# Loading the 128 remainder rows of two weight matrices in sixteen pieces of 15 down to 1 and 8 partitions instead of one piece of 128

## The chip, the cores and the metric

The kernel runs on one core of one Trainium2 chip. The metric is the device time of one execution in microseconds. Each profile is of one execution, and its span (first to last instruction) is some 1.8 us shorter than the device time.

## The reference

Two branches are computed from the same two normalised tokens and added: attention of one new token over the last 2048 positions of a cache (16 key/value heads, 32 query heads, two sequences), and a two-layer MLP with a squared ReLU.

```python
# x [2, 1, 576]; k_cache, v_cache [2, 16, 8192, 128]; wq [576, 4096]; wo [4096, 576]; w1 [576, 4608]; w2 [4608, 576]; all bf16
xn = _layernorm(x)
# branch A
q = (xn @ wq) ...                      # 32 heads of 128
k, v = caches[:, :, Sk - W:, :]        # W = 2048
o = softmax(q k^T / sqrt(128)) v;  A = o @ wo
# branch B
h = relu(xn @ w1 + b1) ** 2;       B = h @ w2 + b2
return x + A + B
```

Some 53.6 MB are read from HBM, the chip's main memory, for two tokens of output, so this is above all a program of loads.

## The kernel before

The inner size 576 is 4 x 128 + 64. The first 512 rows of `wq` and `w1` load as four tiles of 128 rows each. The last 64 rows are folded: each row is cut in two halves, which gives 128 half rows of 2048 elements (wq, 4096 bytes) or 2304 elements (w1, 4608 bytes), one for each of the 128 partitions of SBUF, the memory on the chip that the engines compute from. This folded tile is "the remainder", `wq_rem` and `w_rem` in the profile.

```python
    def issue_kv(tiles, cache, u, name, parts=1):
        tl = kvpool.tile([P, UE], BF16, tag="kv", name=f"{name}_{u}")      # 2 MiB, six buffers
        ...
        return [lambda i=i: nc.sync.dma_start(out=tl[:, i * n:(i + 1) * n], in_=v[:, :, i * n:(i + 1) * n]) ...]

    def issue_w(tiles, wt, c, name, width, lrem):
        if c < NFULL:
            tl = wbig.tile([P, WBW], BF16, tag="wbig", name=f"{name}_{c}")
            nc.sync.dma_start(out=tl[:, 0:width], in_=wt[c * P:(c + 1) * P, :])
        else:
            tl = wrem.tile([P, WRW], BF16, tag="wrem", name=f"{name}_rem")
            nc.sync.dma_start(out=tl[:, 0:lrem], in_=wt[NFULL * P:D, :].rearrange("r (s l) -> (r s) l", s=S))
        tiles[c] = tl
```

Nearly all loads are issued by one engine, SP (`nc.sync`), in this order at the start:

```python
    k0 = issue_kv(k_tiles, A_k_cache, 0, "k", parts=2)
    issue_wq(0); k0[0](); issue_wq(1); k0[1]()
    for c in range(2, KC):        # wq_2, wq_3, then the remainder
        issue_wq(c)
    ...
    load_k(1); issue_w1(0); issue_w1(1); load_v(0); load_k(2)
    for c in range(2, KC):        # w1_2, w1_3, then the remainder
        issue_w1(c)
    load_v(1); issue_wo(0); load_k(3)
```

The framework gives each load a completion semaphore (a counter that tells when the load has landed).

## Time and profile before

| | before |
|---|---|
| device time, median of 2 runs | 137.37 us (137.30 to 137.44) |
| span of the profiled run | 135.6 us |
| packets of the load queue q1, share of 16 engines' span | 94.7%, or 128.4 us of 135.6 |
| the rest of the span (engines idle, or on other queues) | 7.2 us |

The share of a queue, times the span, is the time that an average DMA engine spends in packets of that queue. (A packet is what one engine moves at a time, here one row of one partition: 128 packets of 4096 bytes for the remainder of wq.) 0.947 x 135.6 = 128.4 us. What is left, 7.2 us, holds the start, the end, the instruction fetches and all idleness.

SP's timeline of the kernel before (start, length, line, operation, out<-in, count) around the two remainder loads:

```profile
4.34 0.44 SPq L103 DMA_DIRECT2D wq_rem<-in_A_wq_dram  x1
4.83 0.55 SPq L94 DMA_DIRECT2D k<-in_A_k_cache_dram  x1
10.25 4.59 SPq L100 DMA_DIRECT2D w<-in_B_w_dram  x2
...
21.19 0.42 SPq L103 DMA_DIRECT2D w_rem<-in_B_w_dram  x1
25.88 0.55 SPq L94 DMA_DIRECT2D v<-in_A_v_cache_dram  x1
```

The 2 MiB load of k follows the remainder of wq within 0.5 us, while the engines are still busy with loads from before. And the chain that ended last, by engine (shares of the span):

```profile
DMA 55%; PE 35%; DVE 3%; issue 2%; POOL 1%; ACT 1%; SPq 1%; POOLq 0%; ACTq 0%
```

SP's own issuing is 1% of that chain. And one line of SP's waits (engine and line, releaser: total us, times, longest):

```profile
SPq L94 <- DMA v<-in_A_v_cache_dram: 8.6, 2, 4.3
```

Line 94 issues the k and v loads. So even before the change, some loads wait until an earlier load has landed.

### The profile page before, as it was taken

The page shows a single profiled execution, that of the slowest core. Times are in us where ns is not written, and L with a number is a line of the kernel's source. Part 1 is how long each engine was busy: PE and PEld are TensorE (multiplying, and loading weights), DVE is VectorE, ACT ScalarE, POOL GpSimd, SP SyncE. Part 2 cuts the span into 40 slices and gives each one's busy share as a digit, 9 for nine tenths or more (in the row PEclk, how much of TensorE's full clock was granted, in tenths as well). Part 3 has the DMA queues.
Part 4 walks back from the last instruction along what each step waited for, and adds up shares of the span by engine and source line. Part 5 has one row for each costly group of instructions (what it writes and reads, how often), then busy time and mean ns, then how long its engine had stood idle before and what let it go on. Part 6 is the DMA issues. An engine that isn't in the chain of part 4 may idle for free.

```text
span 135.6 us, 4461 instructions
## 1 busy us (share of the span) xinstructions
PE 102.5 (76%) x2054; PEld 91.9 (68%) x2054; DVE 53.9 (40%) x124; ACT 43.0 (32%) x47; POOL 10.0 (7%) x31
## 2 busy tenths in 40 slices
PE   1049947599968999879943993999399599768961
PEld 0039947589968999839933993688399479664530
DVE  7502421574352325422653446355634645660001
ACT  6705550165012521004701550272155127110000
POOL 6400000110110001100011001101100110110000
PEclk9999985569855685556985698698559959955599
DMA  5999999999999999999999999999999999999940
GB/s 112 418 419 418 428 442 402 420 429 440 430 393 430 438 411 409 444 425 396 440 440 406 445 420 425 404 443 423 425 430 413 430 415 426 422 410 417 393 166 1
DMA packets 5278, 53.90 MB, mean 397 GB/s; under 512 B 630, under 2 KB 652, under 8 KB 1164
## 3 DMA queue, kind: packets, MB, share of 16 engines
q1 hardware_dynamic: 5188, 53.61, 94.7%
q8 instruction: 16, 0.26, 0.8%
q0 software_dynamic: 64, 0.01, 0.0%
q14 instruction: 2, 0.02, 0.0%
q10 hardware_dynamic: 8, 0.00, 0.0%
HBM read 53.62 MB, written 0.00 MB: 395 GB/s over the span
## 4 chain that ended last, share of the span: by engine, by line
DMA 55%; PE 35%; DVE 3%; issue 2%; POOL 1%; ACT 1%; SPq 1%; POOLq 0%; ACTq 0%
DMA k<-in_A_k_cache_dram 41%; PE kT_ps L237 18%; DMA w<-in_B_w_dram 10%; PE hT_ps L323 5%; DMA b_sb<-in_B_b_dram 4%; PE sc_ps L252 4%; PE out_ps L213 4%; PE oT_ps L289 3%; PE qT_ps L225 1%; ACT kT L240 1%; POOL b_sb L146 1%; DVE l L271 1%; DVE sub L266 1%; SPq L94 0%; DVE fin_sb L414 0%
## 5 line engine op out<-in xcount | busy, mean ns | idle before, releaser
L237 PE MATMUL kT_ps<-ident,k 128*128 128x128 bf16 x512 | 47.3, 260 | 9.9 <-DMA k<-in_A_k_cache_dram 9.9
L237 PEld LDWEIGHTS <-k 128*128 128x128 bf16 x512 | 39.6, 119 | 11.8 <-DMA k<-in_A_k_cache_dram 10.7
L240 ACT COPY kT<-kT_ps 128x1024 bf16<-128x1024 bf16 x32 | 32.3, 1012 | 40.1 <-PE kT_ps L237 40.0
L242 DVE COPY kT<-kT_ps 128x1024 bf16<-128x1024 bf16 x32 | 22.0, 690 | 33.4 <-PE kT_ps L237 33.4
L252 PE MATMUL sc_ps<-qT_all,kT 128*128 128x8 bf16 x512 | 21.6, 168 | 1.6 <-ACT kT L240 0.8
L252 PEld LDWEIGHTS <-kT 128*128 128x128 bf16 x512 | 19.1, 100 | 2.6 <-ACT kT L240 1.2
L289 PE MATMUL oT_ps<-pT,v 128*128 128x8 bf16 x512 | 15.5, 167 | 1.9 <-issue 1.4
L269 ACT ACTIVATE pT<-sub 128x512 bf16<-128x512 f32 x8 | 5.0, 630 | 35.1 <-DVE sub L266 35.1
L289 PEld LDWEIGHTS <-v 128*128 128x128 bf16 x512 | 14.4, 99 | 2.1 <-issue 1.6
L271 DVE TENSOR_REDUCE l<-pT 128x8 f32<-128x512 bf16 x8 | 8.5, 1066 | 4.2 <-ACT pT L269 4.2
L213 PE MATMUL out_ps<-wo,ws 128*2 128x288 bf16 x64 | 8.3, 438 | 2.4 <-DVE ws L309 2.4
L323 PE MATMUL hT_ps<-xnT,w 128*128 128x2 bf16 x144 | 9.8, 201 | 0.0
L323 PEld LDWEIGHTS <-w 128*128 128x128 bf16 x144 | 9.4, 165 | 0.0
L258 DVE TENSOR_REDUCE m<-sc_ps 128x8 f32<-128x512 f32 x8 | 5.5, 692 | 9.7 <-PE sc_ps L252 9.7
L262 POOL PARTITION_ALL_REDUCE gmax<-m x8 | 2.9, 364 | 84.8 <-DVE m L260 84.8
L213 PE MATMUL out_ps<-w,hT_sb 128*2 128x288 bf16 x72 | 6.9, 353 | 1.3 <-DMA w<-in_B_w_dram 1.3
L213 PEld LDWEIGHTS <-ws 128*2 128x2 bf16 x64 | 3.5, 115 | 5.4 <-DVE ws L309 2.8
L213 PEld LDWEIGHTS <-hT_sb 128*2 128x2 bf16 x72 | 3.8, 103 | 4.3 <-issue 1.9
L266 DVE TENSOR_TENSOR sub<-sc_ps,gm 128x512 f32<-128x512 f32 x8 | 5.5, 692 | 0.3
L225 PE MATMUL qT_ps<-xnT,wq 128*128 128x2 bf16 x128 | 4.0, 165 | 2.2 <-DMA wq<-in_A_wq_dram 1.9
L225 PEld LDWEIGHTS <-wq 128*128 128x128 bf16 x128 | 3.9, 103 | 2.2 <-DMA wq<-in_A_wq_dram 2.0
L273 POOL PARTITION_ALL_REDUCE lsum<-l x8 | 3.2, 398 | 24.5 <-DVE l L271 24.5
(58 smaller groups left out, 35.1 us busy)
## 6 DMA issues: line engine op xcount, KB each, us to landing
v<-in_A_v_cache_dram SPq DMA_DIRECT2D x8, 2048.0 KB, 28.4
k<-in_A_k_cache_dram SPq DMA_DIRECT2D x7, 2048.0 KB, 29.4
w<-in_B_w_dram SPq DMA_DIRECT2D x4, 1152.0 KB, 17.7
wo<-in_A_wo_dram SPq DMA_DIRECT2D x4, 1152.0 KB, 27.4
wq<-in_A_wq_dram SPq DMA_DIRECT2D x4, 1024.0 KB, 6.9
w<-in_B_w_dram SPq DMA_DIRECT2D x3, 1296.0 KB, 22.7
k<-in_A_k_cache_dram SPq DMA_DIRECT2D x2, 1024.0 KB, 9.1
w<-in_B_w_dram SPq DMA_DIRECT2D x1, 864.0 KB, 15.7
```

The costliest lines, as they stand in the source:

```text
L213: nc.tensor.matmul(out_ps[32 * i:32 * i + B, :], lhsT=lhsT, rhs=rhs_of(i * OH, (i + 1) * OH), start=start, stop=stop, skip_group_check=True)
L225: nc.tensor.matmul(qT_ps[:, h, :], lhsT=lhsT, rhs=xnT[:, xc, :], start=(c == 0 and h == 0), stop=(c == KC - 1), skip_group_check=True)
L237: nc.tensor.transpose(out=kT_ps[:, i * P:(i + 1) * P], in_=k_sb[:, j * Dh:(j + 1) * Dh], identity=ident[:])
L240: nc.scalar.copy(out=kT[:], in_=kT_ps[:])
L242: nc.vector.tensor_copy(out=kT[:], in_=kT_ps[:])
L252: nc.tensor.matmul(sc_ps[:, g * JG + i, :], lhsT=kT[:, i * P:(i + 1) * P], rhs=qT_all[:, b, tq * NC:(tq + 1) * NC], start=True, stop=True)
L258: nc.vector.tensor_reduce(out=m1[:], in_=sc_ps[:].rearrange("p j c -> p c j"), axis=AX.X, op=ALU.max)
L266: nc.vector.tensor_tensor(out=sub[:], in0=sc_ps[:], in1=gm2[:].unsqueeze(1).to_broadcast([P, NJ, NC]), op=ALU.subtract)
L269: nc.scalar.activation(out=pT[:], in_=sub[:], func=ACT.Exp, scale=scale)
L271: nc.vector.tensor_reduce(out=l1[:], in_=pT[:].rearrange("p j c -> p c j"), axis=AX.X, op=ALU.add)
L289: nc.tensor.matmul(oT_ps[:], lhsT=v_sb[:, j * Dh:(j + 1) * Dh], rhs=pT_tiles[u][:, j, :], start=(j == 0), stop=(j == NJ - 1))
L323: nc.tensor.matmul(hT_ps[:, s * FR + r, :], lhsT=lhsT, rhs=xnT[:, xc, :], start=(c == 0 and s == 0 and r == 0), stop=(c == KC - 1), skip_g ...
```

## The change

The intent, as I read it, is to give some DMA engines more rows than others: a load of n partitions, n under 16, is spread over n engines, so loads of 15, 14, ... 1 partitions make a staircase if each begins at the same engine. That they do is my assumption. If some engines finish late for another reason, such a staircase could even them out. The bytes and the matmuls stay the same.

```diff
             tl = wrem.tile([P, WRW], BF16, tag="wrem", name=f"{name}_rem")
-            nc.sync.dma_start(out=tl[:, 0:lrem], in_=wt[NFULL * P:D, :].rearrange("r (s l) -> (r s) l", s=S))
+            rem = wt[NFULL * P:D, :].rearrange("r (s l) -> (r s) l", s=S)
+            p0 = 0
+            for n in list(range(15, 0, -1)) + [8]:
+                nc.sync.dma_start(out=tl[p0:p0 + n, 0:lrem], in_=rem[p0:p0 + n, :])
+                p0 += n
```

More of the change, by code (lines that the diff above doesn't have):

```diff
@@ L360 @@
     load_k(3)
-    nxt = {0: [], 1: [], 2: [lambda: load_v(2), lambda: load_k(4)]}
     def step(u, extra=()):
@@ L404 @@
                 load_k(u + 2)
-        if u >= NU - 1:
-            pass
         if u == NU - 1:
```

## The prediction

Passages are cut from the prediction below, and each cut is marked. The sum that the cut terms belong to came to +2.8 us at the end: eight rows of both tensors more for the engine that was assumed to have a row of every piece (8 x 0.33 = 2.6 us), and 30 more semaphore packets of 6 ns (0.2 us). "Engine 0" is that engine; the higher the number of an engine, the fewer of the pieces it was assumed to have, so that engine 8 came out 0.3 us earlier than before and engine 15, with none, 2.6 us. All of this is an assumption. The tiles behind the pieces were put 1.3 us (wq) and up to 2.8 us (w1) later. The packet records of the kernel before show this much: 36 loads of 128 partitions come with 576 semaphore packets, 16 each, and the load of x, of 2 partitions, has two data and two semaphore packets.

> **What bounds the kernel now.** I read the slices of the page first, then the DMA queues, then the chain of waits near the end, then windows around the end, and last the single packet records of the trace. The slices of the kernel before (busy tenths of 40 slices of 3.39 us, and GB/s):
>
> ```profile
> PE   1049947599968999879943993999399599768961
> DMA  5999999999999999999999999999999999999940
> GB/s 112 418 419 418 428 442 402 420 429 440 430 393 430 438 411 409 444 425 396 440 440 406 445 420 425 404 443 423 425 430 413 430 415 426 422 410 417 393 166 1
> ```
>
> The DMA engines are full from the second slice to the thirty-eighth; PE has holes. So the loads set the time, and what I must ask is not "how many bytes" (the change moves the same bytes) but "which of the 16 engines is done last". That is seen at the end. Windows of the kernel before, from 20 us to the landing of the last load (columns: length, busy time and count of PE, PEld, DVE, ACT, POOL, then PE clock, DMA share, GB/s):
>
> ```profile
> 20.00:125.00 105.00, 86.01 (x1813) 79.23 (x1812) 46.07 (x95) 33.17 (x36) 6.10 (x16) 0.71 1.01 423
> 125.00:128.50 3.50, 3.50 (x34) 1.91 (x32) 0.00 (x0) 0.00 (x0) 0.00 (x0) 0.52 0.97 399
> 128.50:131.80 3.30, 2.21 (x36) 1.34 (x32) 0.00 (x0) 0.00 (x0) 0.00 (x0) 1.00 0.52 204
> ```
>
> For 105 us all engines are full at 423 GB/s, which is 26.4 GB/s an engine. Then, in the last 3.3 us, the share is 0.52 and the rate 204 GB/s: half of the engines have nothing left and the other half go on. The finer windows show the step:
>
> ```profile
> 128.00:128.50 0.50, 0.50 (x10) 0.29 (x6) 0.00 (x0) 0.00 (x0) 0.00 (x0) 0.61 0.97 387
> 128.50:129.00 0.50, 0.38 (x8) 0.14 (x3) 0.00 (x0) 0.00 (x0) 0.00 (x0) 1.00 0.68 277
> ...
> 131.00:131.50 0.50, 0.27 (x6) 0.19 (x7) 0.00 (x0) 0.00 (x0) 0.00 (x0) 1.00 0.46 180
> 131.50:132.00 0.50, 0.50 (x12) 0.33 (x7) 0.00 (x0) 0.00 (x0) 0.00 (x0) 1.00 0.19 69
> ```
>
> The program's end hangs on the slower half. The chain of waits, last pieces (start, length, what):
>
> ```profile
> 119.21 13.05 DMA w<-in_B_w_dram
> 132.26 0.04 issue
> 132.30 0.55 PE out_ps L213 x6
> 132.85 0.02 issue
> 132.87 0.45 DVE fin_sb L414
> ```
>
> After the last load lands at 132.26 us only 0.6 us of matmuls and the store remain. So one microsecond on the last engine is one microsecond of the kernel.
>
> Why is one half late, when each load of 128 partitions gives every engine the same bytes? The queue table gives the only other sizeable traffic:
>
> ```profile
> q1 hardware_dynamic: 5188, 53.61, 94.7%
> q8 instruction: 16, 0.26, 0.8%
> ```
>
> 0.8% of 16 x 135.6 us is 17 us for 16 packets, 1.08 us each. In the packet records, one chained to the next by start and end, each of these 16 fetches takes its engine's turn for some 1.06 us and is followed by a slow data packet (1.08 us where 16 KB otherwise takes 0.61), so it costs its engine about 1.5 us. In those records eight chains end between 128.4 and 129.4 us and eight between 131.65 and 131.82: the difference, 3.1 us, is two fetches. So I read: eight engines carry two fetches each, eight carry none. The records don't number the engines. That gap decides this case.
>
> [...]
>
> **The change part by part.** Removed: two loads, of 128 x 4096 bytes (wq) and 128 x 4608 bytes (w1), 8 rows of each on every engine. Added: 16 loads in place of each, of 15, 14, ... 1 partitions and a last one of 8. [...]
>
> One row of both is 8704 bytes, at 26.4 GB/s 0.33 us. [...] Each small load also ends in a 4-byte semaphore packet; they hold an engine for about 6 ns[...].
>
> SP issues 30 more loads. The old remainder issues took 0.44 and 0.42 us; at up to 0.4 us each, 15 more are at most 6 us at each of two places. In the timeline wq's remainder is issued at 4.34 us and lands 16.6 us later, w1's at 21.2 and lands 27.1 us later: the queue ahead of these issues is 16 and 27 us deep, so 6 us of issuing hides and no engine should run dry. All other engines keep their order: the instruction order of PE, DVE, ACT and POOL is the same but for line numbers.
>
> Intermediate waits: [...] The first stretch of the chain waits for a k tile issued at 15.5 us that lands at 41.2 us; the projections have slack there. The last w2 issue, at 119.2 us, has 13 us of queue ahead of it. So these delays shift work but add nothing at the end beyond engine 0's own lateness.
>
> **The rivals.** It comes down to which eight engines carry the fetches.
> - A: engines 8 to 15. The late ones get less: engine 8 ends at 131.7 - 0.3 = 131.4 us. The early ones get more: engine 0 ends at 128.5 + 2.8 = 131.3. Gain about 0.3 us: 137.1 us. For it: someone who unloads high engines may have seen them late[...].
> - B: a set that holds engine 0 (0 to 7, the even ones, or mixed). Engine 0 ends at 131.7 + 2.8 = 134.5: 140.2 us, 2.1% slower. For it: nothing in the trace forbids it. If the lowest of the set is 1 or 2, +7 or +6 rows, 139.5 to 139.9, within 2%.
> - C: the small loads are badly overlapped, SP can't keep the queue full, or the waits between small semaphores add up; a hole of 1 to 3 us in the DMA row near 11 or 28 us would follow, 138.5 to 140 us. The queue depths speak against it.
> - D: a large gain. Ruled out by the sum: if all 16 engines ended together they would end at (128.7 + 131.7)/2 = 130.2, 1.5 us sooner, 1.1%. No order of rows can give 2%.
>
> **Range and chances.** A I hold at about a half, B with engine 0 at a quarter, its milder forms (engines 1 to 7 alone) at 0.15, C at 0.1. A is "same". B with engine 0 lies at 2.1%, on the edge, and is "slower" in somewhat over half; C in a third. That makes slower about 0.2, faster 0.01. The middle of the chances is just above A: 137.5 us. Because the outcomes have two peaks (137.1 and about 140), the range is wide: 136.7 to 140.4.
>
> **What would show it.** Windows over the last 3 us: in A the share falls in a slope instead of a step and the last load lands at about 132.0; in B the share falls to 0.06 to 0.3 for the last 2 to 3 us, since engine 0 and a few neighbours go on alone, and lands near 135. [...] SP's lines should show 32 remainder issues at 0.1 to 0.4 us, and the DMA row should keep its nines. Wrong would be: fetches that move to other engines, [...](a load of 1 partition spread on 16), or a hole in the DMA row.

## The result, and the profile after

The changed kernel takes 151.14 us (150.89 and 151.39, two runs), against 137.37 us. The ratio is 1.0996, 95% interval 1.0956 to 1.1036: 10% slower, far outside the predicted range. (Ratios here and below, with their intervals, are not quite the ratio of the medians that I quote.)

The slices of the changed kernel, 40 of 3.73 us:

```profile
PE   1079722539994999717399179779979879957751
DMA  4999925999999933999999999999999999999930
GB/s 157 412 420 426 342 55 166 404 403 446 422 435 412 350 72 115 404 400 442 422 418 448 426 422 426 431 399 453 422 422 422 422 406 446 408 414 413 408 150 1
```

Two holes stand in the DMA row that was all nines before: slices 6 and 7 (about 18.6 to 26 us) and slices 15 and 16 (about 52 to 60 us). Everywhere else the rate is what it was. The queues:

```profile
q1 hardware_dynamic: 5412, 53.61, 87.6%
q8 instruction: 16, 0.26, 0.7%
```

0.876 x 149.1 = 130.6 us of packets: 2.2 us more than before. The rest is 18.5 us: 11.3 us more. The sum, 13.5 us, is the growth of the span. So the loss is in two terms of very unequal size, and the larger one is idleness. The packet count tells also that the pieces are spread as intended: 5412 - 5188 = 224 packets more. That fits one semaphore packet for each engine that takes part in a load: two loads of 16 made 32, and the pieces make 2 x (15 + 14 + ... + 1 + 8) = 256, which is 224 more. In the packet records the last nine pieces of wq, of 8, 7, ... 1 and 8 rows, begin in groups of 8 (21.35 to 21.41 us), 7 (21.69 to 21.75), 6, 5, 4, 3, 2, 1 and 8 row packets; the packets of each group all overlap in time (those of the first take 258 to 316 ns), so a piece of n runs on n engines.

The first hole in steps of a microsecond (windows of the changed kernel: length, busy time and count of PE, PEld, DVE, ACT, POOL, then PE clock, DMA share, GB/s):

```profile
17.00:18.00 1.00, 0.83 (x33) 0.74 (x30) 0.69 (x1) 0.98 (x2) 0.00 (x0) 1.00 0.92 295
18.00:19.00 1.00, 0.00 (x0) 0.00 (x0) 0.00 (x0) 0.91 (x1) 0.00 (x0) 1.00 0.74 135
19.00:20.00 1.00, 0.00 (x0) 0.00 (x0) 0.00 (x0) 0.00 (x0) 0.00 (x0) 0.65 0.27 74
20.00:21.00 1.00, 0.51 (x19) 0.51 (x19) 0.00 (x0) 0.00 (x0) 0.00 (x0) 0.50 0.01 4
...
23.00:24.00 1.00, 0.00 (x0) 0.00 (x0) 0.00 (x0) 0.00 (x0) 0.00 (x0) 0.50 0.16 53
24.00:25.00 1.00, 0.00 (x0) 0.00 (x0) 0.00 (x0) 0.00 (x0) 0.00 (x0) 0.50 0.92 250
```

In the window from 20 to 21 us the sixteen engines together move 4 GB/s. They have nothing to do. SP's timeline says what SP does in the meantime:

```profile
4.26 19.05 SPq L106 DMA_DIRECT2D wq_rem<-in_A_wq_dram  x16
23.35 0.55 SPq L94 DMA_DIRECT2D k<-in_A_k_cache_dram  x1
...
27.56 30.11 SPq L106 DMA_DIRECT2D w_rem<-in_B_w_dram  x16
57.72 0.55 SPq L94 DMA_DIRECT2D v<-in_A_v_cache_dram  x1
```

Sixteen pieces of wq occupy SP from 4.26 to 23.3 us, and the k load behind them, issued at 4.83 us before, goes out at 23.35 us. Sixteen pieces of w1 take 30 us, and the v load behind them moves from 25.88 to 57.72 us. The issuing is not what takes this long: a piece takes 0.25 to 0.54 us. SP waits, and its list of waits names for what (engine and line, releaser: total us, times, longest):

```profile
SPq L106 <- DMA k<-in_A_k_cache_dram: 13.6, 4, 4.6
SPq L106 <- DMA w<-in_B_w_dram: 11.3, 4, 4.0
SPq L106 <- DMA wq<-in_A_wq_dram: 9.0, 4, 4.4
```

The line that issues remainder pieces waits for other, earlier loads to land. In the kernel before, the remainder line has no such wait in this list. The chain that ended last, by engine, and its pieces around the first hole (start, length, what):

```profile
DMA 68%; PE 17%; SPq 9%; issue 2%; DVE 1%; ACT 1%; POOL 0%; ACTq 0%; POOLq 0%
```

```profile
3.78 16.67 DMA wq<-in_A_wq_dram
20.46 0.27 SPq L106
20.73 0.04 issue
20.78 0.29 SPq L106
...
23.04 0.27 SPq L106
23.31 0.04 issue
23.35 0.55 SPq L94
```

SP has gone from 1% to 9% of the chain. The chain reads: the last big load of wq lands at 20.46 us; only then SP may issue nine more pieces, one every 0.32 us; only after them comes k. Between 18 and 24 us there is nothing left in the engines' queues but those pieces.

The end, which the prediction was about, costs hardly more than it did, but its shape is another. Windows of the changed kernel:

```profile
142.00:142.50 0.50, 0.00 (x0) 0.00 (x0) 0.00 (x0) 0.00 (x0) 0.00 (x0) 1.00 0.65 263
143.00:143.50 0.50, 0.50 (x14) 0.36 (x9) 0.00 (x0) 0.00 (x0) 0.00 (x0) 1.00 0.42 166
143.50:144.00 0.50, 0.27 (x6) 0.06 (x1) 0.00 (x0) 0.00 (x0) 0.00 (x0) 1.00 0.20 69
144.50:145.00 0.50, 0.39 (x8) 0.28 (x9) 0.00 (x0) 0.00 (x0) 0.00 (x0) 1.00 0.18 69
```

Before, the DMA share stood near 0.5 for two microseconds and then fell; here it slopes down, and about three engines (0.18 of 16) go on alone until 145 us. What the share lacks to 1, summed over half microseconds, is 1.8 us from 128 to 132 us before and 1.9 us from 141 to 145 us here. Neither sign that the prediction gave for its cases A and B can be read from this shape: the kernel with even pieces below (e3) ends in the same way, with 0.64, 0.60, 0.30, 0.12, 0.12 and 0.11 in the half microseconds from 144 to 147 us.

### The profile page after: what moved, and what is told of

The parts are those of the page before. It is cut to its first block, busy times and chain, and to the rows that moved or that the text cites. A ratio compares the mean times of both kernels' runs of the same rounds, so it can differ in the third digit from the quotient of the medians. Undisturbed runs are those within 1.5% of the kernel's fastest.

```text
span 149.1 us, 4499 instructions
## 1 busy us (share of the span) xinstructions
PE 103.3 (69%) x2054; PEld 93.9 (63%) x2054; DVE 54.2 (36%) x124; ACT 43.2 (29%) x47; POOL 10.0 (7%) x31
## 3 DMA queue, kind: packets, MB, share of 16 engines
q1 hardware_dynamic: 5412, 53.61, 87.6%
## 4 chain that ended last, share of the span: by engine, by line
DMA 68%; PE 17%; SPq 9%; issue 2%; DVE 1%; ACT 1%; POOL 0%; ACTq 0%; POOLq 0%
DMA k<-in_A_k_cache_dram 29%; DMA w<-in_B_w_dram 28%; DMA wq<-in_A_wq_dram 11%; PE kT_ps L241 11%; SPq L106 3%; PE sc_ps L256 3%; SPq L94 2%; PE oT_ps L293 2%; SPq L100 2%; PE out_ps L217 2%; SPq L127 1%; ACT kT L244 1%; DVE sub L270 0%; DVE fin_sb L415 0%; POOL gmax L266 0%
## 5 line engine op out<-in xcount | busy, mean ns | idle before, releaser
L241 PE MATMUL kT_ps<-ident,k 128*128 128x128 bf16 x512 | 49.5, 267 | 13.6 <-DMA k<-in_A_k_cache_dram 13.6
L241 PEld LDWEIGHTS <-k 128*128 128x128 bf16 x512 | 41.5, 123 | 15.5 <-DMA k<-in_A_k_cache_dram 14.5
L256 PEld LDWEIGHTS <-kT 128*128 128x128 bf16 x512 | 19.7, 101 | 2.2 <-ACT kT L244 1.0
L217 PE MATMUL out_ps<-w,hT_sb 128*2 128x288 bf16 x72 | 5.4, 299 | 2.8 <-DMA w<-in_B_w_dram 2.8
L217 PEld LDWEIGHTS <-hT_sb 128*2 128x2 bf16 x72 | 3.3, 89 | 4.9 <-issue 3.4
```

The lines of the kernel that those rows point to most:

```text
L217: nc.tensor.matmul(out_ps[32 * i:32 * i + B, :], lhsT=lhsT, rhs=rhs_of(i * OH, (i + 1) * OH), start=start, stop=stop, skip_group_check=True)
L241: nc.tensor.transpose(out=kT_ps[:, i * P:(i + 1) * P], in_=k_sb[:, j * Dh:(j + 1) * Dh], identity=ident[:])
L256: nc.tensor.matmul(sc_ps[:, g * JG + i, :], lhsT=kT[:, i * P:(i + 1) * P], rhs=qT_all[:, b, tq * NC:(tq + 1) * NC], start=True, stop=True)
```

## The experiments

**The first theory** (T1, "lanes", in the expectations). The list of the built program's SP instructions shows, behind each load, the completion semaphore that it waits for:

```
DMACopy wq_rem 15x2048
DMACopy wq_rem 14x2048   waits DMAHW0
DMACopy wq_rem 13x2048   waits DMAHW1
...
DMACopy wq_rem  8x2048   waits DMAHW6      <- the semaphore of wq_3, the last big load
DMACopy wq_rem  7x2048   waits DMAHW7
...
DMACopy k      128x8192  waits DMAHW7
```

The loads that SP and ACT issue take eight semaphores in turn, and a load can be issued only when the load eight places before it has landed. So at most eight loads are in flight. (The traces of both kernels agree: the records of these loads name eight semaphores in turn, and in the changed kernel the eighth piece, issued at 20.46 us, waits for that of wq_3, which landed then.) Eight big ones are 16 us of work or more (in the kernel before, the remainder of wq lands 16.6 us after its issue); eight pieces are next to nothing. When 16 pieces stand in a row, the eighth must wait for the last big load, and by then the engines are empty. This wait is not in the diff: the framework puts it in.

The rivals at first were the uneven rows themselves, and a fixed cost of each small load. The uneven rows come in two sizes: T2, that they cost some 13 us, in proportion to rows, and T3, the +2.8 us of the prediction. Later experiments brought in a second effect, called T4 below. Passages are cut from the expectations, and marked. Other letters or numbers in the texts are explained by the sentence in which they stand.

Every kernel below gave a correct result. All times are medians of four runs, and the kernel before ran in the same rounds on the same chip (137.34 to 137.41 us).

### One remainder at a time

```diff
-            for n in list(range(15, 0, -1)) + [8]:
+            for n in (list(range(15, 0, -1)) + [8] if name == "wq" else [P]):     # e1; e2: "w1"
```

> Only wq's remainder is cut into 16 loads; w1's is one load as before. Theory T1 (each load of the queue waits for the landing of the load eight places earlier, so 16 small loads in a row let the big loads drain and leave the DMA engines empty for some 5 us at each of the two places): one hole near 18 to 24 us, none near 53 us, 143 us (142 to 145). Rival T2 [...]: 47% of the loss by bytes, 143.5 us, but with no hole and a longer tail. Rival T3 (the prediction's sum for the imbalance alone): 137 to 138.8 us.

> Only w1's remainder is cut. T1: no hole near 20 us, one hole of some 5 us near 45 to 55 us, 143 us (142 to 145), and the excesses of e1 and e2 add up to about the whole 13.8 us. T2: 53% of the loss, no hole. T3: 137 to 138.9 us.

Measured: 144.44 us with wq alone cut (ratio 1.0517, 1.0501 to 1.0533), 145.23 us with w1 alone cut (1.0565, 1.0535 to 1.0596). Each profile has one hole, at the place of its own pieces (DMA rows of e1 and e2):

```profile
DMA  4999934899999999999999999999999999999930
DMA  4999999999999259999999999999999999999920
```

The rest of the span grows by 5.9 and 6.2 us, the packets by 1.0 and 0.9 us. The two growths in time, 7.0 and 7.8 us, add up to 14.8 against 13.8 for both: two nearly independent losses.

### The same bytes on every engine

```diff
+            half = lrem // 2
+            for p0 in range(0, P, 16):
+                for h in range(2):
+                    nc.sync.dma_start(out=tl[p0:p0 + 16, h * half:(h + 1) * half],
+                                      in_=rem[p0:p0 + 16, h * half:(h + 1) * half])
```

> Again 16 loads for each remainder, but of 16 partitions by half a row each, so that all 16 engines get the same bytes. T1: the count is the same, so the loss stays: 150 to 153 us with both holes. T2 and T3: no imbalance is left, 137.4 us (137 to 138).

Measured: 152.58 us (1.1113, 1.1087 to 1.1139), both holes. Sixteen pieces that load every engine alike (if a piece of 16 partitions runs on 16 engines, as those of 8 and fewer run on as many) are as slow as the staircase, or a little slower. The uneven rows are not what costs 14 us.

### Pieces with almost no bytes

The remainder stays whole, and 15 loads of 64 bytes into a scratch tile follow it.

```diff
+            nc.sync.dma_start(out=tl[:, 0:lrem], in_=rem)
+            for i in range(15):
+                nc.sync.dma_start(out=scratch[i:i + 1, :], in_=rem[i:i + 1, 0:32])
```

> The kernel before, each remainder in one load of 128 partitions, with 15 loads of 64 bytes to an unused tile after it. Bytes and balance are those of before; only the count of loads is the changed kernel's. T1: 148 to 152 us with both holes. T2 and T3: 137.4 us (137 to 138).

Measured: 150.00 us (1.093, 1.0908 to 1.0951). SP's timeline, and the DMA row of the slices:

```profile
4.74 18.38 SPq L107 DMA_DIRECT2D scratch<-in_A_wq_dram  x15
23.16 0.55 SPq L95 DMA_DIRECT2D k<-in_A_k_cache_dram  x1
```

```profile
DMA  5999914999999914999999999999999999999930
```

Thirty loads of 64 bytes, 2 KB in all, cost 12.6 us. The k load waits until 23.16 us, nearly as in the changed kernel, and both holes are there. The packets grow by 0.8 us only. This shows the idleness with nothing else changed: it needs neither the bytes, nor their division.

### The same tiny loads, not in a row

Thirty loads of 64 bytes again, two behind each big load instead of fifteen behind each remainder.

```diff
+    def two():
+        for i in (next(tiny), next(tiny)):
+            nc.sync.dma_start(out=scratch[i:i + 1, :], in_=A_wq[i:i + 1, 0:32])
     ...
         issue_wq(c)
+        two()
     load_k(1)
+    two()
     issue_w1(0)
+    two()                       # and so on behind each load, cut here
```

> The kernel before with thirty loads of 64 bytes to an unused tile, as in e4, but two after each big load instead of fifteen in a row. T1: of any eight loads in a row at least two are big, so nothing drains[...]: 137.4 us (137.2 to 138.4), the DMA row keeps its nines. If the count of loads itself costs (about 0.4 us for each, as 12.6 us for 30 in e4): 150 us.

Measured: 138.03 us (1.0065, 1.0027 to 1.0104). The DMA row has no hole:

```profile
DMA  4999999999999999999999999999999999999940
```

The same thirty loads cost 12.6 us in a row and 0.7 us spread. So it is not a cost of each load, and SP's issuing hides: the order of the loads alone makes the hole. That settles the first theory for tiny loads.

### Fewer pieces: eight, and four

```diff
-            for n in list(range(15, 0, -1)) + [8]:
+            for n in [16] * 8:          # e5;  e6: [32] * 4
```

> Each remainder in 8 loads of 16 partitions (one row on each engine for each load). T1: the eighth load still waits for the last big weight load to land, but the next k or v load can follow at once, 8 x 0.34 us = 2.7 us sooner than in the changed kernel at each place. The two places lost 7.0 and 7.8 us; so 137.4 + 4.3 + 5.1 = 146.8 us (145 to 148.5). Rival (the loss goes with the count of loads, so much for each load): half of 13.8, 144.3 us. T2, T3 (imbalance): 137.4 us.

> Each remainder in 4 loads of 32 partitions. T1: the k and v loads after them wait for loads that land long before the queue is empty, so no hole: 137.4 us (136.8 to 138.8). Rival (so much for each load): a fifth of the loss, 3 of 15 added loads, 140.2 us.

Measured: eight pieces 147.07 us (1.071, 1.0689 to 1.073), close to what was expected, and in the term that the theory is about: the rest grows by 6.8 us, where the two holes less the saving that was named give 5.9 + 6.2 - 2 x 2.7 = 6.7. (The packets grow by 3.1 us; the second theory below is about those.) Four pieces 142.64 us (1.0383, 1.0366 to 1.04), where the theory of lanes said 137.4 us and its rival, a fixed cost per load, 140.2 us. Both missed. The slices of the kernel with four pieces:

```profile
DMA  3999999999999999999999999999999999999820
GB/s 134 408 413 424 418 281 392 407 458 404 420 424 416 273 295 401 443 417 420 414 434 434 438 410 420 428 413 451 434 406 413 435 411 446 402 421 414 356 114 1
```

There is no hole: the DMA row is nines throughout. But in three slices the busy engines move only 281, 273 and 295 GB/s. The packets grow by 3.6 us and the rest by 1.4 us. Something makes packets slow here, and the theory of lanes has nothing to say on it. In the packet records a remainder row of 4096 bytes takes 160 ns on average in the kernel before and 264 ns here (4608 bytes: 180 and 320 ns).

**The second theory** (T4). These pieces go to bands of neighbouring partitions. T4 says that a load into few neighbouring partitions makes its own packets slow, and those of the loads beside it. The reason that I had for it at the time is not shown by any run; what is tested below is where the rows land. Of the 3.6 us here, about 2.0 are in the remainder rows themselves, as an estimate from their packets (128 rows of each tensor, 104 and 140 ns longer, over 16 engines).

### Four pieces of all 128 partitions

```diff
+            qt = lrem // 4
+            for i in range(4):
+                nc.sync.dma_start(out=tl[:, i * qt:(i + 1) * qt], in_=rem[:, i * qt:(i + 1) * qt])
```

> Four loads for each remainder as in e6, but each over all 128 partitions and a quarter of the row. Theory T4 [...]: [...]137.4 us (137.0 to 138.4), packets at full rate. T5 (what is slow is a small compact region of HBM for all engines at once): also 137.4. Rival, loss for each load: 142.6 as e6.

Measured: 138.35 us (1.0073, 1.0056 to 1.009). The packets have not grown at all (128.4 us), the rest by 1.0 us. Four loads are not slow as such.

### Narrow in SBUF, or narrow in HBM

Two kernels with four pieces of 32 rows. In one, each piece goes to 32 neighbouring partitions and its rows lie four apart in HBM; in the other, each piece is 32 neighbouring rows of HBM and goes to every fourth partition. The copy that prepares x is permuted so that the result stays right.

```diff
+            for q in range(4):                                                              # e10
+                nc.sync.dma_start(out=tl[32 * q:32 * (q + 1), 0:lrem], in_=rem[q::4, :])
+            for q in range(4):                                                              # e11
+                nc.sync.dma_start(out=tl[q::4, 0:lrem], in_=rem[32 * q:32 * (q + 1), :])
```

> Four loads of 32 neighbouring partitions as in e6, but their rows lie four apart in HBM (x is permuted to match, so the result stays right). T4: partitions are as narrow as in e6, 142.6 us (141.5 to 143.5), row packets near 300 ns. T5: the region in HBM is wide, 137.4 us, row packets near 160 and 180 ns.

> Four loads, each to every fourth partition, from 32 neighbouring rows of HBM (x permuted to match). T4: [...]137.4 to 139 us, row packets near 160 and 180 ns. T5: compact in HBM as in e6, 142.6 us, row packets near 300 ns.

Measured: 142.98 us (1.04, 1.0377 to 1.0423) for neighbouring partitions, 137.62 us (1.0021, 1.0006 to 1.0036) for every fourth. The slices of the latter:

```profile
GB/s 114 418 421 423 418 442 402 427 426 435 425 406 412 443 420 413 439 420 411 434 415 449 420 430 415 408 443 440 406 444 394 439 416 435 417 406 409 396 158 1
```

Nothing dips; a row of 4096 bytes takes 159 ns again, where it takes 284 ns with neighbours. What counts is where the rows land in SBUF, and not where they lie in HBM.

### The changed kernel's pieces, not in a row

The pieces of the change exactly as they are, but two behind each big load.

```diff
+                parts.append(lambda a=p0, z=p0 + n: nc.sync.dma_start(out=tl[a:z, 0:lrem], in_=rem[a:z, :]))
     ...
     issue_wq(0)
+    some("wq", 2)               # issues the next two pieces
     k0[0]()
+    some("wq", 2)               # and so on behind each load, cut here
```

> The very loads of the changed kernel, 15 to 1 partitions and 8, two of them after each big load instead of sixteen in a row. T1: of any eight loads in a row at least two are big, so the DMA row keeps its nines; what is left is the imbalance of the rows alone, which the prediction put between 137.1 us (fetches on engines 8 to 15) and 140.3 us (a fetch on engine 0). T2 (imbalance costs 13 us) or loss for each load: 149 to 152 us.

Measured: 147.58 us (1.0738, 1.0715 to 1.0762), where the theory of lanes said 140.3 us at most. Another miss. The page of this kernel:

```profile
DMA  4999999999999999999999999999999999999930
GB/s 135 347 335 358 344 367 394 380 381 319 404 341 350 330 335 363 398 381 405 376 422 433 426 426 426 428 408 434 431 426 417 413 420 437 423 409 411 388 142 1
...
q1 hardware_dynamic: 5412, 53.61, 94.3%
```

The holes are gone, as the theory of lanes says they must. But for as long as pieces are being loaded, some 70 us, the full engines move only 319 to 405 GB/s. 0.943 x 146.0 = 137.7 us of packets, 9.3 us more than before; the rest has grown by 1.1 us only. The loss has changed its column. The packet records add a surprise: the pieces' own rows account for 0.7 us of the 9.3 (198 and 225 ns each). 8.5 us are in the packets of the big loads beside them (mean of a 16384-byte packet 647 ns against 618, of an 8192-byte one 378 against 332, of a 9216-byte one 395 against 352).

### Two pieces, one of them on seven engines

```diff
+            for n in [119, 9]:
```

> Imbalance without many loads: each remainder in two loads, of 119 partitions (should use 7 engines, 17 rows each) and of 9 (one row on each of 9). [...] T1: no hole. Fetches on engines 0 to 6: 140.7 us. Fetches only on higher ones: the early engines end at 128.5 + 3.3 = 131.8, so 137.5 us. T2: 15 us or more lost.

The 3.3 us in it are ten rows of both tensors (10 x 0.33 us) more on each of seven engines; which engines was my assumption.

Measured: 147.35 us (1.0733, 1.0679 to 1.0788), against 140.7 or 137.5. This was meant to measure the uneven rows alone and did not: the packets grew by 6.5 us as well (rows of 301 and 330 ns), although one piece covers 119 partitions. The rest grew by 3.7 us, and the end of the DMA row slopes:

```profile
DMA  4999999999999999999999999999999999998410
```

119 is 7 x 17, and 5188 packets, as many as before, fit a piece of 119 on seven engines of 17 rows and one of 9 on nine (2 x (7 + 9) = 32 semaphore packets). The slope shows that unevenness of that size, in rows and in the time of each, does reach the end. But a narrow band of partitions doesn't explain slow packets of a 119-partition load; seven engines writing all of it may be another way to be slow. This run doesn't show which it is.

### The staircase on every fourth partition, spread and in a row

The row counts of the change, each piece on every fourth partition. In e13 two behind each big load, in e15 sixteen in a row.

```diff
+            for q, ns in enumerate(([15, 14, 3], [13, 12, 7], [11, 10, 9, 2], [8, 8, 6, 5, 4, 1])):
+                a = q
+                for n in ns:
+                    z = a + 4 * (n - 1) + 1
+                    parts.append((n, lambda a=a, z=z: nc.sync.dma_start(out=tl[a:z:4, 0:lrem], in_=rem[a:z:4, :])))
+                    a += 4 * n
+            parts.sort(key=lambda x: -x[0])
```

> The changed kernel's numbers of rows (15 down to 1, and 8), with both costs taken away: each load goes to every fourth partition[...] (T4), and two loads follow each big load instead of sixteen in a row (T1). What is left is the imbalance of the rows, the only cost that the prediction counted. Fetches on engines 8 to 15 (its case A): 137.1 us, with the 0.7 us that e12's spread loads cost up to 138. Fetch on engine 0 (its case B): 140.2 us, up to 141. If the row packets are again near 300 ns, T4 is not cured by the stride and the run says nothing of A and B.

> The changed kernel[...]: the same sixteen loads in a row, each to every fourth partition. T1 alone must then leave the two holes: 149 to 151.5 us. [...]

Measured: spread 142.74 us (1.0391, 1.0374 to 1.0408), packets +4.7 us, rest +0.7 us. In a row 155.90 us (1.1352, 1.1328 to 1.1376), packets +1.4 us, rest +17.0 us. Both are above the ranges expected, by 1.7 and 4.4 us. SP's timeline of the latter, and the line of its tile (count: duration ns min/median/max):

```profile
4.34 21.38 SPq L112 DMA_DIRECT2D wq_rem<-in_A_wq_dram  x16
25.77 0.61 SPq L94 DMA_DIRECT2D k<-in_A_k_cache_dram  x1
```

```profile
L112 SPq DMA_DIRECT2D wq_rem<-in_A_wq_dram x16: 414/718/987, 4.3 to 25.3; - x16
```

In a row the widest pieces give the slowest kernel of all. Issuing one takes SP 718 ns in the median, against 292 ns for a piece of neighbours in the changed kernel. The last nine pieces of wq, issued while the engines run empty, take from 19.6 to 25.8 us, 6.2 us, against 2.9 us in the changed kernel (20.46 to 23.35). Twice the difference, for two holes, is 6.6 us; the rest grew by 5.7 us beyond the changed kernel's.

The four combinations side by side, as growth of packets and of the rest over the kernel before:

| staircase | in a row | two behind each big load |
|---|---|---|
| neighbouring partitions | the change: +2.2, +11.3 us | +9.3, +1.1 us |
| every fourth partition | +1.4, +17.0 us | +4.7, +0.7 us |

The two costs don't add. I read this so that a hole hides the other cost: pieces that land in a hole have no neighbours to slow. The packets agree: a 16384-byte packet takes 624 ns on average in the changed kernel, 647 ns with the same pieces spread, and 618 ns before.

### Half of the partitions at once, the rest in small pieces

```diff
+            parts = [lambda: nc.sync.dma_start(out=tl[0::2, 0:lrem], in_=rem[0::2, :])]
+            for q in (1, 3):
+                for a in range(q, P, 32):
+                    parts.append(lambda a=a: nc.sync.dma_start(out=tl[a:a + 29:4, 0:lrem], in_=rem[a:a + 29:4, :]))
```

> Each remainder in one load of 64 partitions (every second one[...]) and eight of 8 partitions (every fourth one[...]), spread between the big loads[...]. Case A: engines 8 to 15 end 1.3 us sooner, the others 1.3 us later, 136.1 to 137 us, the only version that would beat the kernel before. Fetches on engines 0 to 7: 138.7 to 139.5 us. Fetches on a mixture of both halves: 138.7 us too.

The 1.3 us in it are four rows of both tensors (4 x 0.33 us) moved from one half of the engines to the other. They rest on an assumption of mine that no run shows, that all the small pieces go to the same eight engines.

Measured: 141.33 us (1.0286, 1.0254 to 1.0317), slower than every case that I had written down. Packets +1.8 us, rest +2.0 us. This was the attempt at what the change intends, an engine balance by unequal rows, and was meant to be without the two costs found; with packets 1.8 us longer it is not quite. It didn't beat the kernel before, and neither did any other.

### The same eight rows on neighbours, on every fourth and on every sixteenth partition

Every fourth partition had only halved the slowing (packets +4.7 us, against +9.3). So I kept the size of the pieces (8 partitions, 8 engines), two behind each big load, and changed only which eight partitions a piece takes. The last one is the widest.

```diff
+            for a in range(0, P, 8):                                                  # e16
+                parts.append(lambda a=a: nc.sync.dma_start(out=tl[a:a + 8, 0:lrem], in_=rem[a:a + 8, :]))
+            for a in [h + q for h in range(0, P, 32) for q in range(4)]:              # e17
+                parts.append(lambda a=a: nc.sync.dma_start(out=tl[a:a + 29:4, 0:lrem], in_=rem[a:a + 29:4, :]))
+            for a in range(16):                                                       # e18
+                parts.append(lambda a=a: nc.sync.dma_start(out=tl[a:a + 113:16, 0:lrem], in_=rem[a:a + 113:16, :]))
```

> [...] This run and the next two have the same 32 small loads of 8 partitions each, on 8 DMA engines each, two after each big load (so no dry queue is expected), and differ only in which 8 partitions a load writes. Here 8 neighbours[...]. [...] Spread theory: also the worst, so this run alone tells nothing; it is the anchor.

> Every 4th partition of 32 neighbours[...]. [...] Spread theory (what counts is the span of partitions): in the middle of the three, since these 8 span 32 partitions and those of the next run all 128.

> Every 16th partition of all 128: the widest span[...]. [...] Spread theory: the best of the three, at or under the run with every 4th of 32. [...]if engines 8 to 15 carry the instruction fetches (case A of the prediction), the time in which engines stand idle grows by under 0.5 us against the kernel before; if any of 0 to 7 does, by about 2.7 us.

The last two figures in the text on e18 assume that all pieces go to the same eight engines, which no run shows.

Measured: neighbours 149.04 us (median of three runs; ratio 1.0854, 1.0811 to 1.0897; a fourth run, 174.99 us and the profiled one, was slow, so its profile isn't read); every fourth 144.87 us (1.0536, 1.0507 to 1.0564), packets +5.8, rest +2.1 us; every sixteenth 149.05 us (1.0851, 1.081 to 1.0892), packets +8.7, rest +3.0 us. The slices of the kernel with every fourth and of that with every sixteenth:

```profile
GB/s 131 423 369 389 391 349 411 348 351 425 422 416 398 354 358 359 357 371 363 404 424 427 425 429 411 433 414 437 420 432 420 418 409 442 408 426 412 357 95 1
```

```profile
GB/s 145 370 360 367 348 388 356 359 363 375 408 351 353 339 379 410 360 351 389 380 431 431 423 427 423 411 415 442 432 423 418 424 410 435 405 419 405 259 54 1
```

The spread of the partitions would have made the kernel with every sixteenth the best of the three. It is 2.9% slower than the one with every fourth. So the distance between partitions alone is refuted. Neighbours are no worse than every sixteenth (149.04 and 149.05 us), and even with every fourth partition packets grew by 5.8 us. What makes one set of eight partitions slower than another is not shown.

A rival stands untested: a piece of eight rows runs on eight engines (eight overlapping packets in the changed kernel, at 21.35 us), and it may be the small number of engines that slows packets. With every fourth partition a piece's own row of 4096 bytes takes 174 ns (160 before), so nearly all of the growth is in the packets of the big loads (645 ns for 16384 bytes, 618 before). The means of that packet in the runs without holes sort by the size of the pieces as well as by where they land: 617 and 618 ns beside four pieces of 32 rows on every fourth partition and four over all 128 (e11, e9) and 619 beside 64-byte loads, which move hardly any bytes (e12); 632 and 636 beside four pieces of 32 neighbouring partitions (e6, e10); 625 to 650 beside pieces of under 16 partitions, wherever they land, and beside the pair of 119 and 9 (e7, e8, e13, e14, e17, e18). Only e10 against e11 holds the size fixed: there the destination in SBUF alone makes the difference, of 5.4 us. How much of the slowing in the changed kernel's pieces is due to where they land, and how much to the few engines, is not shown.

## Why the prediction was wrong, point by point

- **What bounds the kernel.** Right in what it says of the kernel before, and still true of the changed one: the last load lands at 145.6 us and 0.6 us of matmuls and the store follow. But "one microsecond on the last engine is one microsecond" made me look at the end alone, and the 11.3 us were lost before 60 us.
- **As many engines as partitions.** Right: 224 packets more, as counted, and 8, 7, ... 1 packets at once for the pieces of 8 down to 1.
- **SP's issuing.** The count (32) and the length (0.25 to 0.54 us each) were right. The step that failed is what followed: "the queue ahead of these issues is 16 and 27 us deep, so 6 us of issuing hides and no engine should run dry". It took the issue times as the whole cost and the depth as given. Each issue also waits for the load eight places earlier, so the depth shrinks with every piece: when the eighth is let go, at 20.46 us, the last big load has landed and the depth is zero. Worth +11.3 us in the changed kernel, +11.8 with 64-byte pieces. My check of the program's order before predicting listed instructions but not their waits; with the waits, the eight semaphores stood there to be read, and SP's waits in the profile before had loads waiting for loads (8.6 us for v on line 94).
- **The cost of a row.** A missing term. The sum took every row at 26.4 GB/s an engine, 0.33 us for both tensors, wherever it lands. In the changed kernel a row of 4096 bytes takes 251 ns instead of 160, and one of 4608 bytes 289 instead of 180; the packets grew by 2.2 us in all. The term is small here only because most of it falls in the holes: without them it is 9.3 us.
- **Rival C.** The right direction, and with the sign that I named ("SP can't keep the queue full"), but sized at 1 to 3 us in all and given a chance of 0.1, on the argument of the queue depths that failed. It was two holes, of 5.9 and 6.2 us when alone, later than the places that I gave (18 to 24 and 52 to 59 us, not 11 or 28).
- **The uneven rows, A or B.** Not settled. The prediction had -0.3 or +2.8 us. Where pieces don't meet holes, the rest of the span, which would hold any unevenness, grows by 1.1 us (neighbours) and 0.7 us (every fourth), less than B with engine 0. With pieces of eight rows alone it grows by 2.1 and 3.0 us, where I had written under 0.5 for A and 2.7 otherwise; that speaks against A only if all pieces begin at the same engine, on which all these sums rest and which no run shows. No run separates unevenness of rows from packets that are slower on some engines, and in the changed kernel itself both holes let the engines run empty, so a lead that an engine had before them can't be seen after them. Nothing numbers the engines.
- **Rival D.** Right as far as seen: nothing that I tried was faster than before.

What stays open: which engines carry the instruction fetches; which engines take the pieces; why packets of the big loads slow down beside small ones (the kernels with neighbours and with every sixteenth partition take 149.04 and 149.05 us, and packets grow by 5.8 us even with every fourth); whether pieces on few engines slow the others; and how the 119-partition piece gets rows of 301 ns.

## What to carry to other kernels

When one load becomes many, list the waits of the built program, not only its instructions: if loads share a handful of completion semaphores, a row of small ones lets the queue run dry, and the same small loads placed between big ones cost 0.7 us instead of 12.6. Split loads along the free dimension over all partitions, or over every fourth partition, and not into bands of neighbours: here four full-width pieces cost 0.7%, four pieces on every fourth partition 0.2%, four bands 3.8%. And split a slowdown first into time in packets and time without, by the queue's share and the span: here that one product told two causes apart that looked alike in the total.
